# A long convolution and an MLP block on one core: new buffer plan and work order, and the second filter spectrum folded by accumulated matmuls

## The chip, the cores and the metric

The kernel runs on one core of a Trainium2 chip. The metric is device microseconds of one execution. The five engines (TensorE = PE, VectorE = DVE, ScalarE = ACT, GpSimd = POOL, SyncE = SP) each work through a queue of their own in order; SP issues almost all DMAs. A semaphore wait at the head of a queue holds everything behind it.

## What is computed

```
x  = q                                          # 2048 x 512, bf16
kv = (4-tap causal shift of k by shift_k) * v
y  = first 2048 of ifft(fft(kv, 4096) * fft(ssm_k, 4096)) + kv * ssm_D
h  = x + layernorm(x) * y
u  = layernorm(h);  g = gelu(layernorm(u) @ w1)
x1 = u + (g, its four column quarters shifted by -1, +1, -2, +2 rows) @ w2
out = h + x1 + gelu(layernorm(x1) @ w3) @ w4    # w3: 512x1792, w4: 1792x512
```

## The kernel before

**Two halves.** The rows form two halves s = 0, 1 of 1024 rows, each of eight blocks b of 128. The FFT of length 4096 is done as two steps of small matmuls against sine tables. Four signals go forward: the filter's halves F0 and F1, and kv's halves A0 and A1. The first output half needs A0·F0, the second A0·F1 + A1·F0.

**The work calls.** Every call is registered once with a name, its dependencies and a function; a string `ORDER` (lines 31 to 62) lists all calls by number, with the engine letter (P, V = DVE, A = ACT, G = POOL, S = SP) and the PSUM banks. `emit` walks the string, so ORDER alone sets each engine's queue. The names used below:

- convolution, forward: `S1.sig.b.hp` step 1 on PE (line 397, eight 128x32 matmuls of 512 columns, four column groups side by side), `E1` its eviction to SBUF (line 266, 128x1024), `X.sig.g.kl` an SBUF to SBUF transposition by DMA (line 412), `S2.sig.kl` step 2 on PE (line 420), `E2` its eviction. For F1 the eviction is the fold of line 432: it reads the PSUM result and the stored F0 spectrum and writes their difference (real part) or sum (imaginary part), on DVE only.
- kv: `K.g.c` the shift as matmuls with diagonal tables `dg` (line 449), `KV` the product with v (line 457).
- convolution, back: `P.s.kl...` products of spectra on DVE (line 481; 16 for s = 0, 32 for s = 1), `I2.s.kl` inverse step 2 on PE (line 493), `EV` its eviction, `XI.s.kl` DMA (line 503), `I1.s.b` inverse step 1 on PE (line 511).
- gating with q: `Q` statistics (line 516), `Y` normalised q, `H.s.b` the sum h (line 619), `HS` its second moment (line 603 on ACT, 605 on DVE); `uw`, `rr`, `hn` finish the statistics of a pair of blocks, partly on POOL.
- first MLP: `hb` normalised block (line 655 or 653), turned either on PE (`LT`, line 671, then eviction `TE`) or by two DMA writes to DRAM and a transposing DMA back (`LT`, `TE` at lines 664 and 666 on SP); `W.s.p.h` the matmul with w1 (line 700), `U` its gelu, `X2.s.b` the shifted matmul with w2 (line 729), `S` the sum x1 (line 732), `SS` its second moment, `R` the residual (line 736).
- second MLP: `ux`, `r1`, `xn` statistics, `lb` the normalised block, `LX`/`EX` its turn (PE or DMA), `M.s.p.fp` the matmul with w3 (line 781, seven for a pair p of blocks), `G` its gelu, `O.s.b` the matmul with w4 (line 793), `Z` the last sum (line 795), `OUT` the store (line 797).

**Order before.** PE does all of both convolutions up to `I2.1.3`, with `W.0`, `X2.0.0` to `X2.0.5` between, and then `M.0.0.0`, the first matmul of the second MLP; `I1.1` follows behind the seven `M.0.0`.

**Buffers before.** The large buffers are shared in time. z1 (step 1 results) of A0, F1 and A1 all lie in `r_y`, of F0 in `r_x`; z2/spectrum of A1 and `wv[0]` lie in `r_x`, `wv[1]` in `r_y`. Gelu results G rotate over four homes. Turned blocks have two buffers for the first MLP (`hnT`) and two for the second (`lnT`); normalised blocks two `hbt` and two `lbt`. `Z` writes to two output buffers.

Of the kernel before, what the change touches and what calls it, by code (L numbers as in the profile page):

```python
# [9 lines left out]
P = 128  # L10
# [33 lines left out]
391A0 392P71 394A1 395P6 276P 277V0 413G 414G 393A 396A 368A 278V1 262P4567 281V2 415G 401G 253S 402G 403G 280V3 263A 028S 279P 257S 282P 283M 284A
416V0 399P5 400A 384P4 385A 418S 417V1 419S 286V0 268P0123 420S0 264V 269A 397P7 398A 287V1 289V2 270V 404G0 290V3 265P4501 266A 288P23671 291P 406S
423P5 405A1 292V0 424A 293V1 296V2 267A 294P 421P4 295V3 297P 422A 285S 298A 407S 513P5 302V0 301V1 303P01230 304V2 408S0 305V3 306P 299A 509P4 514V
307V0 308V1 411P5 515A 409P7 510V 511A 310V2 311V3 309P 312P 412A 317V0 410A 521P7 313A 300S 314A 517P6 316V1 320V2 319V3 318P01451 522V 321P 322V0
525P3 337S 573G 574G 575G 579A0 576A1 323V1 325V2 577P70 578A 529P2 580P7 315S 326V3 523A 324P 581A 518V 519A 602G 603G 604G 605G0 327P 329A 328A
582P70 588P6 594P5 430V 431V 429V 584P4 426V 585A 330S 583A 425V 592P1 593A 586P0 427V 589A 587A 428V 432V 433V 590P4 591A 526V 530V 434G 527V 606A1
331P76 332P43 333P21 531A 435V 439G0 595A 516V 440V 599P5 436A1 441A 437V 445G0 442G1 630V 438V 446V 451A0 443V 608S 596P0 631G 632G 607S 609S0 600V0  # L50
601S 460G 461G 334P37 444A 447A 473G 452V 448A1 633V0 635S 610P60 614P1 634V1 611A 616P5 620P6 449V 612P4 450V 457G0 453V 454A1 618P2 615A 462G 466A0
613A 617A 458V 622P7 636S 637S1 638P10 644P5 623A 455V 463V1 464P70 465A 621A 459V 619A 524V 640P4 456V 467P3 645A 646P7 474G 475V 477G1 479S 468V
469P6 471P5 497V 520V 498G 624P3 476A0 499V 478S 528V 480S0 472A 470A 500A1 625V0 502S 533P6 534V 485G 501A0 503S 504S1 537P5 538V 648P3 650P6 649A
539A 535V 483P5 484A 486G 487V 642P3 643A 489V0 491S 481P2 647A 488G1 627P5 658G 659G 660G 482A 512V 597V1 532V 662A0 507P7 490S 492S0 641A 661A1 663S
508A 505P4 495P0 493P7 506A 541P4 545P3 626S 546V 639A 494A 496A 553P7 557P2 561P3 651A 549P6 547A 554V 542V 543A 742V 743G 562V 563A 598S 555A 558V
744V 745A1 550V 569P4 565P7 566V 664S 665S0 666P30 667A 674P2 675A 678P6 652P7 655P3 560V 746V0 748S 628V0 672P5 564V 629S 747S 749S1 676P2 570V 571V
750P40 751A 668P1 669A 548V 756P0 551V 757A 686G 687G 688V 677A 690V0 692S 752P4 753A 689V1 552V 673A 670P1 671A 559V 760P2 761A 762P5 691S 714V 715G
716V 754P4 718G0 717V1 693S0 758P2 759A 694P10 696P0 653V0 654S 704P7 719S 568V 679A 705A 680P2 700P7 540V 695A 536V 763A 702P6 698P5 755A 767P4 720S
656V1 567V 657S 699A 701A 770G 771G 697A 706P7 721S1 722P50 772G 773G0 730P3 774G1 731A 556V 776S 724P1 725A 544V 775S 683P0 684V0 777S0 734P3 703A
764P6 707A 778P70 784P1 685S 728P0 785A 735A 765V0 766S 711P6 681V1 782P1 572V 783A 712V0 713S 682S 732P3 733A 726P6 729A 768V0 769S 727A 708P2 709V1  # L60
710S 723A 788P6 789A 739P5 740V0 741S 790P6 786P4 791A 787A 780P5 781A 736P6 737V0 738S 779A 792P7 793V1 794S 795P6 796V0 797S
# [3 lines left out]
class Plan:  # L65
# [4 lines left out]
    def add(self, name, opts, fn, deps=(), take=(), drop=(), size=0, mode=0, port="", mate=None):  # L70
        n = len(self.t)
        t = dict(mate=mate, n=n, name=name, opts=opts, fn=fn, deps=set(), take=list(take), drop=[], size=size, mode=mode, port=port)
        for d in deps:
            t["deps"].add(self.by[d])
        for d, part, *kind in drop:
            m = self.by[d]
            t["deps"].add(m)
            t["drop"].append((m, kind[0] if kind else self.t[m]["take"][0][0], part))
        self.by[name] = n
        self.t.append(t)  # L80
# [20 lines left out]
def body(ctx, tc, fx, kt, q, v, sd, w1, w2, w3, w4, out):  # L101
# [25 lines left out]
    r_dg = raw("r_dg", DC * 4 * P)  # L127
    w4s = raw("w4s", FC * D)[:].rearrange("p (f d) -> p f d", f=FC)
    z_t = ct("z_t", 2, D, dt=F32)
    hnT = ct("hnT", 2, DC, 256)  # L130

    q_sb = r_q[:].rearrange("p (s b d) -> p s b d", s=2, b=NB)
    fxs = view(r_h, 0, G, "p (s b d) -> p s b d", s=2, b=NB)
# [14 lines left out]
    z1 = {"F0": z1v(r_x), "A0": z1v(r_y), "F1": z1v(r_y), "A1": z1v(r_y)}  # L148
    z2 = {"F0": z2v(r_f0), "F1": z2v(r_f1), "A0": z2v(r_a0), "A1": z2v(r_x)}
    sp = {"F0": spv(r_f0), "F1": spv(r_f1), "A0": spv(r_a0), "A1": spv(r_x)}  # L150
    wv = {0: z1v(r_x), 1: z1v(r_y)}
# [3 lines left out]
    h1T = r_h[:].rearrange("p (c b x) -> p c b x", c=DC, b=NB)  # L155
    h_sb = {0: view(r_v, 0, NB * D, "p (b d) -> p b d", b=NB), 1: view(r_a0, 0, NB * D, "p (b d) -> p b d", b=NB)}
    w1s = view(r_v, NB * D, DC * D, "p (k d) -> p k d", k=DC)
    w2s = view(r_v, NB * D + DC * D, DC * D, "p (k d) -> p k d", k=DC)
    w3s = view(r_k, 0, DC * F, "p (k f) -> p k f", k=DC)
    gbq = [[view(r, lo, 2048, "p (f x) -> p f x", f=8) for lo in (0, 2048)] for r in (r_kv, r_x, r_f0, r_f1)]  # L160

    def gb(i, f, n=1):
        u = f // 8
        r, z = ((0, u), (1 + u, 0), (1 + u, 1), (3, u))[i]
        return gbq[r][z][:, f % 8:f % 8 + n, :]
    lbt = view(r_k, DC * F, 2 * D, "p (i d) -> p i d", i=2)
    obt = [r_kv[:, GS:GS + D], ct("ob1", D)[:]]
# [3 lines left out]
    lnT = r_dg[:].rearrange("p (i c x) -> p i c x", i=2, c=DC)  # L171

    ident = ct("ident", P)
    f1 = ct("f1", 8, 2, 2, 2, 4)
    f2 = ct("f2", 4, 32, 4)
    ftab = ct("ftab", 16, 2, 32)
    ttab = ct("ttab", 8, 3, 64)
    hbt = ct("hbt", 2, D)
    junk = ct("junk", D)
    negpi = ct("negpi", 1, dt=F32)  # L180
    mhalf = ct("mhalf", 8, dt=F32)
    dum = ct("dum", 1, dt=F32)
    qst = ct("qst", 16, 6, dt=F32)
    qmv = ct("qmv", 16, 2, dt=F32)
# [96 lines left out]
    for b in range(4):  # L281
        load(("Lf", 0, b), fxs[:, 0, 2 * b:2 * b + 2, :], fx[0, b].rearrange("p (b d) -> p b d", b=2), size=310)
# [398 lines left out]
    def front(s, p):  # L681
# [8 lines left out]
        if dm:  # L690
            turn("hb", "LT", "TE", "hn", lambda k: hbt[:, k, :], lambda k: hnT[:, k], s, p)
# [154 lines left out]
```

## Time and profile before

| what | us |
|---|---|
| median of 3 runs | 222.65 (221.59 to 222.97) |
| span of the profiled execution | 221.2 |
| PE busy | 200.6, 2372 matmuls |
| DVE busy | 145.3, 320 instructions |
| ACT busy | 134.9, 214 instructions |
| POOL busy | 67.3, 187 instructions |
| moved by DMA | 34.47 MB |

The median lies 1.45 us above the profiled span. An instruction's duration in a row is from its start to its end; back to back, instructions of DVE and ACT overlap by some 0.05 to 0.1 us, so a run of n instructions is taken from the start of the first to the start of what follows ("pace" below). Mean duration of one instruction: fold of line 432 on DVE 681 ns (128x512, 16 of them), 128x1024 eviction (line 266) 1.01 to 1.03 us on ACT and 1.21 to 1.23 us on DVE, product (line 481) 694 ns, w3 matmul 273 ns, w4 matmul 379 ns. DMA landings after issue, median: `X` 3.0 to 4.0 us, `XI` 3.5, block write to DRAM 2.0 to 2.1, transposing DMA 3.1, w3 9.2.

### The profile page before, as it was taken

How to read it: one execution, taken by the hardware profiler on the slowest of the kernel's cores; microseconds unless marked ns; L12 is line 12 of the kernel's file. 1: busy time of each engine (PE TensorE's matmuls, PEld its weight loads, DVE VectorE, ACT ScalarE, POOL GpSimd, SP SyncE). 2: the span in 40 equal slices, each digit the busy share in tenths (PEclk: the TensorE clock that was granted, in tenths of full speed). 3: DMA queues.
4: the chain of work that ended last, by engine and by line, in shares of the span. 5: the costliest groups of instructions: out<-in, count | busy, mean ns of one | idle time of the engine just before them, and what ended most of it. 6: DMA issues, size and time to landing. Idle time of an engine off the chain costs nothing.

```text
span 221.2 us, 5913 instructions
## 1 busy us (share of the span) xinstructions
PE 200.6 (91%) x2372; PEld 118.7 (54%) x2372; DVE 145.3 (66%) x320; ACT 134.9 (61%) x214; POOL 67.3 (30%) x187
## 2 busy tenths in 40 slices
PE   6889578996867799999999999999999999999993
PEld 4454234451223255558548958746588666665641
DVE  7898989999499899899899348059765001312121
ACT  4799889988498979687956646655063323123400
POOL 7342000093276680234685345003125000000000
PEclk9999999999695899999999999999999999999998
DMA  6996798869927535973234154341415402111001
GB/s 193 363 394 271 286 291 318 309 244 307 426 115 268 187 83 160 269 303 98 50 74 95 27 113 102 89 104 46 91 32 142 98 2 45 47 50 47 24 24 47
DMA packets 35996, 34.47 MB, mean 156 GB/s; under 512 B 26753, under 2 KB 28802, under 8 KB 35714
## 3 DMA queue, kind: packets, MB, share of 16 engines
q1 hardware_dynamic: 35970, 34.11, 48.6%
q8 instruction: 18, 0.29, 0.6%
q14 instruction: 8, 0.07, 0.1%
HBM read 13.13 MB, written 5.24 MB: 83 GB/s over the span
## 4 chain that ended last, share of the span: by engine, by line
PE 67%; DMA 11%; SPq 6%; ACT 6%; DVE 5%; issue 2%; POOL 0%; DVEq 0%
PE ps L781 22%; PE ps L793 22%; PE ps L729 6%; PE ps L700 5%; PE ps L493 4%; SPq L412 4%; DMA r_h<-in_fx_dram 3%; SPq L275 3%; DMA r_k<-in_kt_dram 3%; DMA r_x<-r_y 3%; PE ps L511 3%; DVE r_f L432 2%; PE ps L397 2%; ACT r_y L266 2%; DMA r_f<-r_y 2%
## 5 line engine op out<-in xcount | busy, mean ns | idle before, releaser
L781 PE MATMUL ps<-r_dg,r_k 128*128 128x256 bf16 x448 | 51.4, 273 | 0.0
L781 PEld LDWEIGHTS <-r_k 128*128 128x128 bf16 x448 | 43.6, 98 | 7.8 <-issue 0.7
L785 ACT ACTIVATE r_f<-ps 128x512 bf16<-128x512 f32 x26 | 14.9, 598 | 27.8 <-PE ps L781 27.8
L793 PE MATMUL ps<-w4s,r_f 128*128 128x512 bf16 x104 | 24.1, 379 | 0.0
L481 DVE TENSOR_TENSOR r_p<-r_a,r_f 128x1024 bf16<-128x1024 bf16 x32 | 20.8, 694 | 1.0 <-PE ps L493 0.9
L266 ACT CAST r_y<-ps 128x1024 bf16<-128x1024 f32 x19 | 18.6, 1022 | 4.6 <-PE ps L397 4.1
L493 PE MATMUL ps<-r_p,ttab 32*32 32x512 bf16 x768 | 15.8, 379 | 1.4 <-ACT r_x L266 0.6
L700 PE MATMUL ps<-hnT,r_v 128*128 128x256 bf16 x128 | 16.5, 281 | 0.5 <-DMA hnT<-dhb 0.5
L795 DVE TENSOR_TENSOR r_kv<-ps,r_v 128x512 bf16<-128x512 f32 x5 | 3.4, 686 | 20.5 <-PE ps L793 20.5
L795 DVE TENSOR_TENSOR r_kv<-ps,r_a 128x512 bf16<-128x512 f32 x6 | 4.2, 692 | 19.3 <-PE ps L793 17.3
L449 PE MATMUL ps<-r_dg,r_k 128*128 128x256 bf16 (+3 forms) x112 | 15.8, 288 | 1.0 <-ACT r_dg L314 0.5
L785 ACT ACTIVATE r_x<-ps 128x512 bf16<-128x512 f32 x16 | 9.2, 599 | 12.2 <-PE ps L781 12.2
L793 PEld LDWEIGHTS <-r_f 128*128 128x128 bf16 x104 | 10.2, 98 | 11.8
L266 ACT CAST r_vs<-ps 128x1024 bf16<-128x1024 f32 (+1 forms) x12 | 14.3, 1228 | 2.4 <-PE ps L493 1.9
L700 PEld LDWEIGHTS <-r_v 128*128 128x128 bf16 x128 | 12.5, 100 | 5.1 <-issue 2.0
L793 PE MATMUL ps<-w4s,r_x 128*128 128x512 bf16 x64 | 15.1, 379 | 0.0
L729 PE MATMUL ps<-r_v,r_h 128*128 128x512 bf16 x64 | 15.0, 380 | 0.0
L449 PEld LDWEIGHTS <-r_k 128*128 128x128 bf16 x112 | 9.5, 98 | 8.9 <-issue 4.6
L266 ACT CAST r_x<-ps 128x1024 bf16<-128x1024 f32 x14 | 13.7, 1017 | 0.7 <-PE ps L397 0.4
L397 PEld LDWEIGHTS <-f 128*32 128x32 bf16 x256 | 6.2, 99 | 12.6 <-issue 7.3
L493 PEld LDWEIGHTS <-ttab 32*32 32x32 bf16 x768 | 8.3, 88 | 8.7 <-issue 6.0
L793 PE MATMUL ps<-w4s,r_kv 128*128 128x512 bf16 x56 | 12.6, 379 | 0.0
(180 smaller groups left out, 343.8 us busy)
## 6 DMA issues: line engine op xcount, KB each, us to landing
r_k<-in_kt_dram SPq DMA_DIRECT2D x8, 259.0 KB, 5.6
r_h<-in_fx_dram SPq DMA_DIRECT2D x8, 256.0 KB, 4.9
r_v<-in_v_dram SPq DMA_DIRECT2D x4, 512.0 KB, 6.2
r_q<-in_q_dram SPq DMA_DIRECT2D x8, 256.0 KB, 6.4
r_f<-r_x SPq DMA_DIRECT2D x8, 256.0 KB, 3.0
r_a<-r_y SPq DMA_DIRECT2D x8, 256.0 KB, 3.5
r_x<-r_vs SPq DMA_DIRECT2D x4, 512.0 KB, 3.5
r_f<-r_y SPq DMA_DIRECT2D x8, 256.0 KB, 4.0
```

Source lines behind the costliest of these rows:

```text
L266: (act.copy if e in "AM" else on[e].tensor_copy)(o, i)
L397: nc.tensor.matmul(ps[32 * j:32 * j + 32, sl[hh], :], lhsT=f1t[:, 4 * t + 2 * hp + hh, :], rhs=src(2 * b + b0), start=True, stop=True)
L412: nc.sync.dma_start(z2[sig][g:P:2, kl, :, :], z1[sig][kl:P:4, 2 * g:2 * g + 2, :, :])
L449: nc.tensor.matmul(o[:, (d + j0) * P:(d + j1 + 1) * P], lhsT=kT[s][c][:, bb, x:x + P], rhs=diag[:, c, j0:j1 + 1, :].rearrange("p j x -> p ...
L481: on[e].tensor_tensor(out=prs[:, sl[0], :, :], in0=sp[a][:, kl, t, :, :], in1=gv, op=MUL)
L493: nc.tensor.matmul(ps[c:c + 32, bk[h], :], lhsT=ttab[32 * h:32 * h + 32, 2 * kl + t, 2 if x else xx, 32 * b0:32 * b0 + 32], rhs=prs[32 * h ...
L700: nc.tensor.matmul(ps[:, sl[0], j * 256:(j + 1) * 256], lhsT=w1s[:, k, m * P:(m + 1) * P], rhs=hnT[:, k_, k, :], start=(k == 0), stop=(k = ...
L729: nc.tensor.matmul(ps[:, sl[0], :], lhsT=h1T[:, m, bb, x:x + P], rhs=w2s[:, m, :], start=(m == 0), stop=(m == DC - 1))
L781: nc.tensor.matmul(ps[:, sl[0], j * 256:(j + 1) * 256], lhsT=w3s[:, k, fc * P:(fc + 1) * P], rhs=lnT[:, k_, k, :], start=(k == 0), stop=(k ...
L785: act.activation(gb(gi, 2 * fp, 2), ps[:, got(("M", s, p, fp))[0], :].rearrange("p (j x) -> p j x", j=2), ACT.Gelu_apprx_tanh)
L793: nc.tensor.matmul(ps[:, sl[0], :], lhsT=gb(gi, fc)[:, 0, (b % 2) * P:(b % 2 + 1) * P], rhs=w4s[:, fc, :], start=(fc == 0), stop=(fc == FC ...
L795: add(("Z", s, b), {V: 0.61}, lambda e, sl, b=b: vec.tensor_tensor(out=obt[sl[0]], in0=ps[:, got(("O", s, b))[0], :], in1=h_sb[s][:, b, :] ...
```

## The change

1. **The fold.** A table `f1g` is built from `f1`: for each pair of cosine and sine columns, (-second, first). Step 1 of F1 takes two sources: the F1 rows with `f1`, and in the same PSUM accumulation the F0 rows with `f1g`. The F1 spectrum then comes out of step 2 already folded; the 16 folds on DVE are gone, and its eviction is an ordinary `E2` copy. F1's step 1 has 16 matmuls a call instead of 8: 64 more.
2. **Buffers.** `r_x`, `r_y` become `r_a1`, `r_z`; `wv[0]`, `wv[1]` and A1's z1 lie in `r_z`, A1's z2 in `r_a1`. F0's source rows have a buffer of their own (later w1 and w2), F1's lie in the second half of q's, so the loads of q's second half wait for F1's step 1. h lies in v's buffer for both halves, `Z` writes in place. Gelu homes go from four to eight places behind six locks; the homes of the first and third pair lie in v's second half, so `I1.1.0` waits for the `O` of these two pairs. The turned blocks share three buffers `xT`, the normalised ones four, across both MLPs.
3. **The h1T buffer** is split into halves, with `ed0` and `ed1` copying the two edge columns that the other half needs, and `edge0`, `edge1` the zero columns.
4. **The turn** of the pairs (0,2) and (0,3) of the first MLP goes from DMA to PE: 16 more transposing matmuls, four `TE` copies; four writes and two transposing DMAs fewer.
5. **ORDER** is new as a whole (804 calls against 798). PE's queue reaches `M.0.0.0` before `S2.F1.3`, `I2.1.2` and `I2.1.3`, which now stand between the matmuls of the second MLP; `I1.1` stands between the `M.0.2`. Of the eight `E2.F1`, six halves of a spectrum go to ACT, two to DVE. The pairs of the second MLP go in the order (0,1), (0,2), (0,0), (0,3) for the choice of homes only.

The core of the diff (without ORDER and renamed buffers):

```diff
-    z1 = {"F0": z1v(r_x), "A0": z1v(r_y), "F1": z1v(r_y), "A1": z1v(r_y)}
-    z2 = {"F0": z2v(r_f0), "F1": z2v(r_f1), "A0": z2v(r_a0), "A1": z2v(r_x)}
-    wv = {0: z1v(r_x), 1: z1v(r_y)}
+    z1 = {"F0": z1v(r_f1), "A0": z1v(r_a1), "F1": z1v(r_a1), "A1": z1v(r_z)}
+    z2 = {"F0": z2v(r_f0), "F1": z2v(r_f1), "A0": z2v(r_a0), "A1": z2v(r_a1)}
+    wv = {0: z1v(r_z), 1: z1v(r_z)}
...
+    def f1turn(e, sl):
+        x, y = (z[:].rearrange("p a i c j k -> p (a i) c (j k)") for z in (f1, f1g))
+        if e == V:
+            vec.tensor_scalar(out=y[:, :, 0, :], in0=x[:, :, 1, :], scalar1=-1.0, scalar2=None, op0=MUL)
...
+        on[e].tensor_copy(y[:, :, 1, :], x[:, :, 0, :])
...
-    def step1(b, hp, src):
+    def step1(b, hp, *srcs):
         def f(e, sl):
             for hh in range(2):
-                for t in range(2):
-                    for b0 in range(2):
-                        j = 2 * t + b0
-                        nc.tensor.matmul(ps[32 * j:32 * j + 32, sl[hh], :], lhsT=f1t[:, 4 * t + 2 * hp + hh, :], rhs=src(2 * b + b0), start=True, stop=True)
+                for i, (src, tab) in enumerate(srcs):
+                    for t in range(2):
+                        for b0 in range(2):
+                            j = 2 * t + b0
+                            nc.tensor.matmul(ps[32 * j:32 * j + 32, sl[hh], :], lhsT=tab[:, 4 * t + 2 * hp + hh, :], rhs=src(2 * b + b0),
+                                             start=(i == 0), stop=(i == len(srcs) - 1))
...
-                if sig == "F1":
-                    def fold(e, sl, n=n, kl=kl, t=t):
-                        for r, op in ((0, SUB), (1, ADD)):
-                            vec.tensor_tensor(out=sp[sig][:, kl, t, r, :], in0=ps[:, got(n)[2 * t + r], :], in1=sp["F0"][:, kl, t, 1 - r, :], op=op)
...
-    BYDMA = {("hb", 0, 2), ("hb", 0, 3), ("hb", 1, 1), ("hb", 1, 2), ("hb", 1, 3), ("lb", 0, 1), ("lb", 0, 2), ("lb", 0, 3),
+    BYDMA = {("hb", 1, 1), ("hb", 1, 2), ("hb", 1, 3), ("lb", 0, 1), ("lb", 0, 2), ("lb", 0, 3),
```

PE's queue around the first matmul of the second MLP, in call names (from the two ORDER strings):

```
before: ... X2.0.4 LX.0.0 X2.0.5 LX.0.1 I2.1.3.2 I2.1.3.3 M.0.0.0 M.0.0.3 ... M.0.0.4 I1.1.0 I1.1.1 I1.1.2 O.0.1 O.0.0 I1.1.3 M.0.1.0
after:  ... X2.0.5 LX.0.0 S2.A1.3 LX.0.1 X2.0.2 M.0.0.0 S2.F1.3 M.0.0.3 ... M.0.0.4 I2.1.2.0 I2.1.2.1 O.0.0 I2.1.2.2 I2.1.2.3 O.0.1 I2.1.3.0 M.0.1.0
        I2.1.3.1 ... M.0.1.6 I2.1.3.2 I2.1.3.3 O.0.3 O.0.2 M.0.2.0 I1.1.0 M.0.2.6 I1.1.1 M.0.2.1 I1.1.2 ... LT.1.0 M.0.2.5 LT.1.1 I1.1.3 W.1.0.1
```

## Prediction

> **What bounds it now.** First the shares by engine and the slices in time, then the chain, then the stretches.
>
> ```profile
> PE 200.6 (91%) x2372; PEld 118.7 (54%) x2372; DVE 145.3 (66%) x320; ACT 134.9 (61%) x214; POOL 67.3 (30%) x187
> ...
> PE   6889578996867799999999999999999999999993
> ...
> DVE  7898989999499899899899348059765001312121
> ACT  4799889988498979687956646655063323123400
> ...
> PEclk9999999999695899999999999999999999999998
> ```
>
> PE has holes in the first 14 slices (77 us) and none later; DVE and ACT are as full there as PE. The shares over the span hide that.
>
> ```profile
> 56.19 1.89 PE ps L511 x8
> ...
> 100.18 6.22 PE ps L781 x56
> 106.40 2.70 PE ps L511 x24
> ...
> 208.42 9.08 PE ps L793 x42
> 217.50 0.02 issue
> 217.52 0.69 DVE r_kv L795
> ```
>
> In the chain, PE runs without a wait from M.0.0.0 (100.18) to its last matmul (217.52): 117.3 us. So the end is the start of M.0.0.0, plus the PE work behind it, plus a tail of 221.2 − 217.5 = 3.7.
>
> ```profile
> 0.00:20.00 20.00, 16.55 (x176) 9.45 (x180) 16.51 (x52) 15.65 (x25) 9.62 (x58) 1.00 0.83 296
> 20.00:40.00 20.00, 15.38 (x300) 6.59 (x292) 18.38 (x23) 17.44 (x19) 0.22 (x1) 1.00 0.86 304
> 40.00:60.00 20.00, 16.73 (x336) 7.32 (x330) 17.53 (x30) 15.23 (x16) 8.25 (x18) 0.91 0.87 323
> 60.00:80.00 20.00, 15.07 (x272) 7.03 (x268) 17.84 (x40) 18.01 (x33) 13.92 (x35) 0.83 0.53 185
> 80.00:100.00 20.00, 19.37 (x491) 10.65 (x488) 18.68 (x34) 16.41 (x27) 5.89 (x14) 1.00 0.69 215
> ```
>
> (Stretch, PE, weight load, DVE, ACT, POOL busy, clock, DMA.) PE idles 3.45 + 4.62 + 3.27 + 4.93 + 0.63 = 16.9 us before 100. To this come slow-clock pieces of the chain: at 56.19 eight matmuls of line 511 take 1.89, later 0.97 (+0.9); 58 us: 16 of line 397 take 1.74 instead of 1.05 (+0.7); 69.8: line 700 1.86 instead of 1.05 (+0.8); two S2 1.06 instead of 0.63 (+0.9). In all 3.3. Lost: 20.2; pure PE work before M.0.0.0: 100.2 − 20.2 = 80.0. From 20 to 100 DVE is busy 72.4 of 80 us (0.905), ACT 67.1 (0.84): these two decide when M.0.0.0 can start.
>
> **The change, PE.** Added: 64 matmuls of S1.F1. Eight of line 397 take 0.50 to 0.55 us in the chain (16 in 1.00, 8 in 0.55), so 8 x 0.52 = +4.2. No row accumulates two passes in line 397's four column groups. At least 0, if they all fill holes (they take PE time, so no gain); 64 x 379 ns = 24.3, if none ran beside another. I take 4.2: I2 (line 493) accumulates in groups of 32 columns and 32 of its matmuls take 0.55. Four more LT at 0.22: +0.9. Moved behind M.0.0.0: I2.1.2 and I2.1.3 (four times 64 matmuls at 1.09 = 4.4) and S2.F1.3 (0.6): −5.0. So before M.0.0.0 there are 80.1 us, as before; behind it 117.3 + 5.0 = 122.3. The break-even is M.0.0.0 at 217.5 − 122.3 = 95.2.
>
> **The fold.** A fold of 1024 columns is two of the 681 ns rows, pace 1.24; the copy that takes its place has pace 1.14 on DVE (three of line 266 from 19.65 to 23.05), 0.92 on ACT. So DVE loses 8 x 1.24 and gets 2 x 1.14 back, −7.6; ACT gets 6 x 0.92 = +5.5. The rule against the change is in the Trainium skill, TensorEngine Tiling (Array Packing), section PSUM Bottleneck: tiling speeds TensorE up but not the emptying of PSUM. The rows agree that this work stays; what is gained is that ACT may do it. By the rule alone, PE's 4.2 would be pure loss: +4.2.
>
> **When M.0.0.0 can start.** It needs EX.0.0 (ACT) and EX.0.1 (DVE). Up to 22.9, where ACT starts on E2.F0 (the first cast to r_f), the loads and KV set the pace; one q load now stands before the last k load, another before the second v load, and the k rows land up to 2 us later (9.9 to 12, at 0.85 us per 256 KB), but the last A0 steps come out at 22 to 23 again, since fewer E1.F0 are left then. I count from 22.9 in both. The `f1g` table is two small DVE instructions (line 316's pace 0.16 to 0.19 for 128x128), 0.35, while DVE waits for k: 0, or 0.35 without that cover.
>
> ACT's queue from there to EX.0.0: 47 evictions x 0.92 = 43.2; 8 U x 0.49 = 3.9; 7 squares x 0.74 = 5.2; 3 scalings x 0.72 = 2.2; 2 copies x 0.49 = 1.0; gelu table 1.4. Sum 56.9: without a gap it ends at 79.8, with the busy share of before (0.84) at 90.7.
>
> DVE's queue to EX.0.1: 33 products x 0.60 = 19.8; 9 evictions x 1.14 = 10.3; 8 KV x 0.615 = 4.9; 7 Q x 0.61 = 4.3; 8 H and 4 S x 0.75 = 9.0; 3 moments x 0.83 = 2.5; 8 turned copies x 0.38 = 3.0; R, three hb, Y 2.3; the small statistics 4.6. Sum 60.7: gapless 83.6, at share 0.905 90.0.
>
> So M.0.0.0 starts between 84 and 91, given 0.5 for PE to get there. PE alone allows 80.1 + 3.4 (the first idle stretch) = 83.5. I take 88.5, above the middle, as neither queue was ever gapless. Before, DVE had all 32 P.1 and eight folds in front; now 15 P.1 stand behind, with I2.1.2 and I2.1.3 under M.0.0 and M.0.1. P.0 shows the gain first: DVE gets to P.0.3 with two KV and one EV between instead of seven KV, two E1 and four Q, so I1.0.0 should start near 48 to 50 instead of 56.19.
>
> **Clock.** After idles of 1.71 and 2.21 us the granted clock of 5 us stretches fell to 0.66 and 0.63. The Trainium skill, TensorE: Matmul & The Clock Gate, Part 1, asks for an idle window of about 3.4 us; here shorter holes in a row sufficed. By the rule none of the 3.3 us would come back; I keep it inside the shares above.
>
> **Behind M.0.0.0.** Counting PE work against the chains:
> - P.1.2 and P.1.3: I2.1.3.2 is reached 22 us after M.0.0.0, DVE has its products at 19. Hidden; each us of DVE beyond 3 is on the path.
> - `ed1` on POOL waits for all P.1 and the U.0.3; behind it r1.0.2, xn.0.2 and lb.0.5 wait, for EX.0.4 and M.0.2.0. It holds them to 19; EX.0.4 lands at 27, PE comes at 29.
> - `ed0` waits for U.1.0, with rr.1.3, hn.1.3 and TE.1.6 behind it. A DMA turn takes 5.7 us from the first write's issue to landing (107.75, transposition issued 110.37, +3.1). TE.1.6 lands near 53.5, PE wants W.1.3 at 52.5: 1 us.
> - I1.1.0 waits for four O that PE did just before: 0. XI.1.3, behind EX.0.4 on SP, lands at 28, PE comes at 30.
> - Three instead of four turned buffers: EX.1.2 must land between X2.1.2 and M.1.1.0, with 11.6 us of PE work between. The chain S, SS, ux, r1, xn, lb (0.75 + 0.74 + 0.65 + 1.0 + 0.6 + 0.8, two S in front) and 5.7 make some 12; before, from X2.1.0's end (144.5) to EX.1.0's landing (155.94 + 3.1) it was 14.6. So 0.5 to 3 us.
> - X.F0.1.2 stands on SP behind the last E1.F0 (ACT, after three sine tables), with Lv.1.1 and the other X.F0 behind it; S2.F0 comes 6 us later: 0. If that cover is gone, 1 to 2 us, inside the shares.
> - Z in place, zero columns, two DMA turns fewer: not on the chain, 0; SP has 2 x 1.2 + 4 x 0.4 us less to issue.
>
> Sum of waits: 0 to 5, I take 1.5. Span 88.5 + 122.3 + 1.5 + 3.7 = 216.0, and 1.45 for the median's distance: 217.5, 2.3% less.
>
> **Rivals.**
> - No difference: M.0.0.0 comes at 90, but the DMA turns in front of W.1.2, W.1.3, M.1.1 and M.1.2 are each late as before's 14.6 us suggest, together 5 us. 90 + 122.3 + 5 + 3.7 + 1.45 = 222.4. For it: the five slacks are under 1 us. Against: no turn held PE for more than 0.5 us before.
> - Slower: ACT becomes the bound. It takes the new copies, and E1.A1 now waits for I1.0, which shares r_z. At the busy share of ACT's worst stretch (15.23 of 20, 0.76), EX.0.0 comes at 22.9 + 56.9/0.76 = 97.8, and 98.3 + 122.3 + 1.5 + 3.7 + 1.45 = 227.3. It makes the kernel over 1% slower once M.0.0.0 is later than 95.2 − 1.5 + 2.2 = 95.9. Against: the wait of 3.09 us at 59 in that stretch was for I1, which now comes earlier.
> - The added pass does not run beside itself: up to +20 us, near 237. Against: I2's row.
>
> **Chances.** Forecast (M.0.0.0 at 84 to 91, waits to 3) 0.64; no difference 0.17; slower by ACT 0.15, by serial matmuls 0.04. Low end 84 + 122.3 + 3.7 + 1.45 = 211.5; high end M.0.0.0 at 93 and 4.5 of waits, 225. One per cent is about what a measurement tells from none; faster 0.64, within 0.17, slower 0.19.
>
> **What would show it.** S1.F1 calls at 1.0 to 1.1 us; I1.0.0 near 49 (later than 54: the P.0 step is wrong); ACT's idle from 23 to M.0.0.0 below 11 us; M.0.0.0 at 84 to 91; then no wait on PE over 3 us. Wrong if M.0.0.0 comes after 95, or PE waits over 5 us behind it.

## The result and the profile after

| what | before | after |
|---|---|---|
| median of 4 runs each, us | 222.47 (221.59 to 222.97) | 228.51 (227.41 to 231.02) |
| ratio, 95% interval | | 1.0276 (1.0221 to 1.0332) |
| span of the profiled execution, us | 221.2 | 226.6 |
| start of `M.0.0.0`, us | 100.18 | 96.12 |
| from there to the end of the last matmul, us | 117.3 | 126.8 |

The kernel became 2.8% slower. `M.0.0.0` starts 4 us earlier, where 11.7 had been forecast, and the stretch behind it is 9.5 us longer, where 6.5 had been forecast with its waits. Runs over 1.5% above the fastest of their kernel are left out of the ratios here and of the medians in the table below, and the profiled executions of e2_sd_early_act, e5_v_early and e6_grouped are such runs, so that only what does not depend on that is read from them.

The page of the changed kernel, its shares by engine and its slices of 5.7 us:

```profile
PE 203.1 (90%) x2452; PEld 118.9 (52%) x2452; DVE 146.1 (64%) x350; ACT 131.5 (58%) x204; POOL 62.5 (28%) x160
...
PE   7099976799869989999999999989998999999993
...
DVE  7377997789699998998966288726897000005321
ACT  3666998979799976985543389134753375500000
...
PEclk9979999999999999999999999999999999999999
```

The second slice of PE is a 0, where before had an 8: for 5 us PE does nothing at all, at the very start. DVE has a hole there too (3, before 8). The clock is full in all slices but the third, so the slow-clock pieces round 75 us are gone, and the time is lost all the same.

The chain of waits shows what stood at the start (start, duration, what):

```profile
1.64 4.07 DMA r_fx<-in_fx_dram
5.73 5.01 DMA r_vs<-in_sd_dram
10.76 0.42 DVE r_fx L299
11.22 2.75 PE ps L403 x13
...
195.73 27.21 PE ps L791 x126
222.96 0.69 DVE r_v L793
```

`r_vs<-in_sd_dram` is `Lsd`, the load of `ssm_D`: 1 KB. It is issued when a 256 KB load of filter rows has landed (1.64 + 4.07 = 5.71), and takes 5.01 us itself. Line 299 is `dr`, which adds `ssm_D` to the first filter row, and `S1.F0.0.0` on PE waits for it. The instructions of this place, with the idle time before them and what ended it in brackets:

```profile
5.73 0.50 ACTq L276 DMA_DIRECT2D r_vs<-in_sd_dram  x1
10.76 0.41 DVE L299 TENSOR_TENSOR r_fx<-r_fx,r_vs 1x512 bf16<-1x512 bf16 x1 [3.12 <-DMA r_vs<-in_sd_dram]
11.22 2.75 PE L403 MATMUL ps<-r_fx,f 128*32 128x512 bf16 x24 [5.36 <-DVE r_fx L299]
```

The load stands on ACT's queue. Before, SP issued it at 3.06 us as the sixth of its loads, and DVE came to `dr` at 9.91 without waiting. In ORDER this is one letter of one word, `000S` to `000A`. The prediction does not mention it.

The stretches of 20 us up to `M.0.0.0` (PE, weight load, DVE, ACT, POOL busy; clock, DMA share, GB/s):

```profile
0.00:20.00 20.00, 13.37 (x125) 7.27 (x126) 12.39 (x44) 12.08 (x18) 11.74 (x63) 0.91 0.76 248
20.00:40.00 20.00, 16.16 (x293) 7.65 (x295) 17.39 (x23) 16.18 (x17) 2.36 (x5) 1.00 0.84 286
40.00:60.00 20.00, 16.54 (x381) 8.00 (x369) 15.96 (x33) 16.74 (x17) 3.17 (x3) 1.00 0.65 209
60.00:80.00 20.00, 17.75 (x309) 8.57 (x307) 19.09 (x57) 19.60 (x31) 15.64 (x28) 1.00 0.69 232
80.00:100.00 20.00, 18.81 (x317) 11.43 (x315) 19.26 (x38) 15.65 (x25) 2.13 (x9) 1.00 0.65 270
```

In the first stretch PE does 3.2 us less than before (16.55), DVE 4.1 less, ACT 3.6 less. From 60 to 80 ACT is busy 19.60 of 20 us and DVE 19.09: that work is dense now, but it came late. The prediction counted from ACT's first cast to `r_f`, and took it at 22.9 as before. Here it is at 27.77; the second row is `EX.0.0` on ACT, for which `M.0.0.0` waits, as for `EX.0.1` on DVE, which ends at 95.97:

```profile
27.77 3.86 ACT L262 CAST r_f<-ps 128x1024 bf16<-128x1024 f32 x4
...
94.31 0.59 ACT L262 COPY r_dg<-ps 128x512 bf16<-128x512 bf16 x1
```

Behind `M.0.0.0`, PE's timeline:

```profile
126.02 1.04 PE L778 MATMUL ps<-xtx,r_k 128*128 128x256 bf16 x8
127.00 1.04 PE L512 MATMUL ps<-r_z,f 64*128 64x512 bf16 x8
127.97 1.05 PE L778 MATMUL ps<-xtx,r_k 128*128 128x256 bf16 x8
128.95 1.04 PE L512 MATMUL ps<-r_z,f 64*128 64x512 bf16 x8
129.92 1.05 PE L778 MATMUL ps<-xtx,r_k 128*128 128x256 bf16 x8
...
151.32 1.92 PE L703 MATMUL ps<-r_dg,r_fx 128*128 128x256 bf16 x16 [0.81 <-DMA r_dg<-dhb]
...
172.71 3.67 PE L778 MATMUL ps<-r_dg,r_k 128*128 128x256 bf16 x32 [0.88 <-DMA r_dg<-dlb]
...
176.82 1.05 PE L778 MATMUL ps<-xtx,r_k 128*128 128x256 bf16 x8 [0.44 <-DMA xtx<-dlb]
```

Two things are new. Eight `M` (line 778, whole array) and eight `I1` (line 512, tiles of 64 rows) that take turns start 0.97 to 0.98 us apart; among themselves eight `M` take 0.87, and eight `I1` 0.90 in before's 24 in 2.70. And three DMA turns come late: from the start of the row before by its pace, PE stands 0.97, 1.04 and 0.62 us there.

### The profile page after: what moved, and what is told of

The parts are those of the page before. It is cut to its first block, busy times and chain, and to the rows that moved or that the text cites. A ratio compares the mean times of both kernels' runs of the same rounds, so it can differ in the third digit from the quotient of the medians.

```text
span 226.6 us, 6041 instructions
## 1 busy us (share of the span) xinstructions
PE 203.1 (90%) x2452; PEld 118.9 (52%) x2452; DVE 146.1 (64%) x350; ACT 131.5 (58%) x204; POOL 62.5 (28%) x160
## 4 chain that ended last, share of the span: by engine, by line
PE 55%; DMA 15%; DVE 12%; issue 6%; ACT 5%; SPq 3%; POOL 2%; DVEq 0%; ACTq 0%; POOLq 0%
PE ps L791 20%; PE ps L778 14%; PE ps L726 5%; PE ps L494 4%; PE ps L403 3%; PE ps L703 3%; DMA r_a<-r_a 3%; DVE r_v L622 2%; DMA r_vs<-in_sd_dram 2%; DMA r_v<-in_v_dram 2%; ACT r_a L262 2%; SPq L419 2%; PE ps L450 2%; DMA r_dg<-dlb 2%; DMA r_fx<-in_fx_dram 2%
## 5 line engine op out<-in xcount | busy, mean ns | idle before, releaser
L793 DVE TENSOR_TENSOR r_v<-ps,r_v 128x512 bf16<-128x512 f32 x16 | 10.8, 685 | 42.4 <-issue 30.3
L778 PE MATMUL ps<-r_dg,r_k 128*128 128x256 bf16 x280 | 32.8, 273 | 1.0 <-DMA r_dg<-dlb 0.9
L262 ACT CAST r_a<-ps 128x1024 bf16<-128x1024 f32 (+1 forms) x23 | 25.1, 1130 | 4.8 <-PE ps L403 3.2
L262 ACT CAST r_f<-ps 128x1024 bf16<-128x1024 f32 (+1 forms) x19 | 19.4, 1063 | 7.5 <-PE ps L403 7.0
L778 PE MATMUL ps<-xtx,r_k 128*128 128x256 bf16 x168 | 20.7, 273 | 0.4 <-DMA xtx<-dlb 0.4
L622 DVE SCALAR_TENSOR_TENSOR r_v<-ps,qsd,z_t 128x512 bf16<-128x512 f32 x16 | 11.4, 747 | 6.4 <-PE ps L512 6.1
L729 DVE SCALAR_TENSOR_TENSOR r_q<-r_v,hrr,ps 128x512 bf16<-128x512 bf16 x16 | 11.6, 742 | 5.3 <-PE ps L726 5.1
L703 PEld LDWEIGHTS <-r_fx 128*128 128x128 bf16 x128 | 12.0, 98 | 4.3 <-issue 1.3
L619 POOL TENSOR_SCALAR z_t<-r_q,qrs,qnm 128x512 f32<-128x512 bf16 x13 | 10.3, 796 | 12.2 <-DVE r_v L622 11.0
L791 PE MATMUL ps<-w4s,r_a 128*128 128x512 bf16 x56 | 12.7, 379 | 0.0
```

Source lines behind the costliest of these rows:

```text
L262: (act.copy if e in "AM" else on[e].tensor_copy)(o, i)
L622: vec.scalar_tensor_tensor(out=h_sb[s][:, b, :], in0=ps[:, got(("I1", s, b // 2))[b % 2], :], scalar=qsd[:, i:i + 1], in1=z_t[:, got(("Y", ...
L703: nc.tensor.matmul(ps[:, sl[0], j * 256:(j + 1) * 256], lhsT=w1s[:, k, m * P:(m + 1) * P], rhs=xt[:, k, :], start=(k == 0), stop=(k == DC ...
L729: vec.scalar_tensor_tensor(out=q_sb[:, s, b, :], in0=h_sb[s][:, b, :], scalar=hrr[:, 4 * s + b // 2, 0, b % 2:b % 2 + 1], in1=ps[:, got((" ...
L778: nc.tensor.matmul(ps[:, sl[0], j * 256:(j + 1) * 256], lhsT=w3s[:, k, fc * P:(fc + 1) * P], rhs=xt[:, k, :], start=(k == 0), stop=(k == D ...
L791: nc.tensor.matmul(ps[:, sl[0], :], lhsT=gb[:, fc, (b % 2) * P:(b % 2 + 1) * P], rhs=w4s[:, fc, :], start=(fc == 0), stop=(fc == FC - 1))
```

## The experiments

In all kernels below, both controls among them, the transposing DMAs are plain DMAs of the same 256 KB in pieces of 256 bytes, so that the blocks which go by that way stay unturned.

```diff
-        nc.sync.dma_start_transpose(
-            xT[sl[0]].rearrange("p c x -> p (c x)"), d[:].rearrange("c p x -> (c p) x")),
+        nc.sync.dma_start(
+            xT[sl[0]].rearrange("p c (h x) -> p (c h) x", h=2), d[:].rearrange("c (h p) x -> p (c h) x", h=2)),
```

| kernel | median (runs), us | ratio to before, 95% | profiled, us | `M.0.0.0` | to last matmul |
|---|---|---|---|---|---|
| c_before | 220.10 (7) | 0.9951 (0.9903 to 0.9999) | 220.10 | 97.21 | 117.4 |
| c_after | 227.63 (2) | 1.0284 (1.0182 to 1.0387) | 226.87 | 95.31 | 125.7 |
| e1_sd_sp | 224.25 (4) | 1.0118 (1.0028 to 1.0207) | 223.77 | 91.69 | 126.4 |
| e4_no_fold_mm | 232.14 (4) | 1.0500 (1.0441 to 1.0558) | 232.17 | 97.74 | 128.1 |
| e2_sd_early_act | 224.31 (7) | 1.0219 (1.0115 to 1.0323) | 227.70 | 104.78 | 117.4 |
| e3_mm_fold_alone | 229.15 (4) | 1.0301 (1.0240 to 1.0362) | 229.44 | 106.35 | 117.6 |
| e5_v_early | 222.45 (9) | 1.0072 (1.0016 to 1.0128) | 225.14 | 93.76 | 125.7 |
| e6_grouped | 224.94 (6) | 1.0136 (1.0086 to 1.0186) | 227.91 | 94.07 | 128.2 |
| e7_sd_act_first | 224.35 (4) | 1.0158 (1.0093 to 1.0224) | 224.34 | 93.27 | 125.4 |
| f1_fill_i1 | 223.04 (10) | 1.0125 (1.0088 to 1.0161) | 222.80 | 91.06 | 126.1 |
| f2_fill_late | 222.78 (11) | 1.0084 (1.0053 to 1.0114) | 222.49 | 91.12 | 125.7 |
| f3_table_later | 221.06 (12) | 1.0021 (0.9986 to 1.0057) | 220.91 | 90.79 | 124.5 |

Each ratio is to runs of the kernel before that were made beside it, so the difference of two kernels by their ratios is not quite that of their medians (up to 1.8 us apart below).

**The controls.**

> Control: the kernel before with its 12 transposing DMAs replaced by plain DMAs of the same 256 KB between the same places (256-byte pieces; the two-block turns are left out, so those blocks enter the matmuls unturned). PE never waited long for a turn here: 222 to 223 us, as before.

> Control: the changed kernel with its 10 transposing DMAs replaced by plain DMAs of the same size (the turns of these blocks are left out). All theories: the start up to M.0.0.0 at 96 is untouched; a plain DMA lands about 1 us earlier, so the waits of 0.8, 0.9 and 0.4 us at the turns shrink: 226.5 to 228.5 us, still 1.5 to 2.5% above the kernel before.

The difference is still there with plain DMAs: 7.5 us between the medians, where the two kernels with the transposing ones differ by 5.7. c_before came 2 us under what was expected of it, c_after as expected, but its median rests on two runs. So the experiments can be made on these two, and a difference to c_after is good to about 1 us.

**The load of ssm_D back on SP.** One letter of ORDER:

```diff
-000A
+000S
```

> As c_after (turns left out), with one word of ORDER altered: the 1 KB load of ssm_D (Lsd) is issued by SP, second in its queue, instead of by ACT. Theory A (the late ssm_D row, landed at 10.7 us, holds DVE and then PE for 5 us and moves everything behind it): the first step 1 of block 0 starts near 7 instead of 11.2 us, M.0.0.0 comes 4 to 5 us earlier (91 to 92), and the kernel is 4 to 5 us faster than c_after. Rival B (the 64 added matmuls are the loss): the start is earlier but PE is full later on, 0 to 1 us faster than c_after. Rival C (the new order is held by v's loads, which SP issues late, and by DMA turns): 1 to 2 us faster than c_after.

224.25, that is 3.4 us below c_after (3.1 by the profiled executions, 3.7 by the ratios): more than rivals B and C give, less than theory A's 4 to 5. The timeline of e1_sd_sp at the start, with idle time and its end in brackets:

```profile
1.17 0.32 SPq L276 DMA_DIRECT2D r_vs<-in_sd_dram  x1
...
7.53 0.41 DVE L299 TENSOR_TENSOR r_fx<-r_fx,r_vs 1x512 bf16<-1x512 bf16 x1
...
7.99 1.48 PE L403 MATMUL ps<-r_fx,f 128*32 128x512 bf16 x24 [1.60 <-DVE r_fx L299]
```

SP issues the load at 1.17, `dr` runs at 7.53 without a wait for it, and PE starts on `S1.F0.0.0` 3.2 us earlier than in the changed kernel. `M.0.0.0` comes 3.6 us earlier than in c_after, at 91.69, just outside the forecast's 84 to 91. This one word holds a little under half of the 7.5 us; some 4 us against c_before remain. By the profiles they arise behind `M.0.0.0`: it comes 5.5 us earlier than in c_before, and from there to the last matmul it takes 9.0 us more, of which 4.8 are the calls that were moved there.

**The same load on ACT in the old order.** The opposite edit in c_before:

```diff
-000S
+000A
```

> c_before with one word of ORDER changed: the 1 KB load of ssm_D (Lsd) is issued by ACT instead of SP, at the same place in the order. At that place its completion counter has no earlier user, so that ACT issues it right after its sines, at about 2.7 us (c_before: SP at 3.05, and dr, which needs it, at 9.81 without waiting for it). Theory A1 (in the changed kernel the load was late because it had to wait for the counter of a slower load, issue 5.73, and then stood behind the loads that were issued before it): issued at about 2.7 it lands before 9.8, dr stays at 9.8, the time is that of c_before, 220.8, within 1 us. Theory A2 (a small load that ACT issues lands late as such, 5 us or more behind the loads of SP, wherever it stands): it lands at 8 to 10.5, dr at up to 10.5, the time 220.8 to 221.8.

224.31, 4.2 us above c_before (5.9 by the ratios). Neither theory's issue time came: in e2's timeline ACT comes to the load only behind four evictions,

```profile
4.67 3.76 ACT L268 CAST r_x<-ps 128x1024 bf16<-128x1024 f32 x4
...
9.72 0.50 ACTq L282 DMA_DIRECT2D r_vs<-in_sd_dram  x1
...
13.74 0.41 DVE L305 TENSOR_TENSOR r_h<-r_h,r_vs 1x512 bf16<-1x512 bf16 x1 [3.98 <-DMA r_vs<-in_sd_dram]
14.21 1.04 PE L399 MATMUL ps<-r_h,f 128*32 128x512 bf16 x8 [2.26 <-DVE r_h L305]
```

It stands from 8.43 to 9.72 at the issue itself, and the 1 KB lands 4.0 us after it. The program's list of instructions has, for this issue as for that of the changed kernel, a wait on the completion counter of an earlier load: the loads of all queues use eight counters in turn, and here the issue waits for counter 7. In the changed kernel it is counter 2, that of SP's third load, the 256 KB of filter rows in the chain above. So the place in the queue, the counter and the landing add up, and the load costs 3.4 us in the new order and 4 to 6 in the old one.

**The load first on ACT.** This tells the queue from the counter and the backlog:

```diff
+    act.dma_start(drow[0:1, :], sd)
     vec.memset(wup, 0.0)
...
-    add("Lsd", {SP: 0.42, A: 0.5}, lambda e, s: (nc.sync if e == SP else nc.scalar).dma_start(drow[0:1, :], sd), size=16)
+    add("Lsd", {SP: 0.42, A: 0.5}, lambda e, s: None, size=16)
```

> c_after with the 1 KB load of ssm_D still issued by ACT, but as the first instruction of its queue, ahead of the load of ACT's table; there its completion counter has no earlier user and no other load is under way (c_after: the load waits for the counter of a 256 KB load, is issued at 5.73 and lands behind the loads issued before it). Theory A1 (wait for the counter and the backlog make it late, not the queue): issued at about 0.8, dr at 7.5 and the first matmuls of S1.F0.0 at 8.0 as in e1_sd_sp; time that of e1_sd_sp, 223.5 to 225. Theory A2 (a small load that ACT issues lands late wherever it stands): landing after 9, time 226 to 229.4.

224.35, as e1_sd_sp. In its timeline the load is issued at 0.71 and `dr` no longer waits:

```profile
0.71 0.51 ACTq L210 DMA_DIRECT2D r_vs<-in_sd_dram  x1
...
7.84 0.41 DVE L300 TENSOR_TENSOR r_fx<-r_fx,r_vs 1x512 bf16<-1x512 bf16 x1
```

Theory A1 holds: ACT's queue as such is not slow. What counts is that the load is issued before the others and waits for none of them. How the counter's wait and the landing behind the other loads share the cost was not separated.

**The fold undone.** e1_sd_sp with the eight folds on DVE again and one source in F1's step 1:

```diff
-    forward1("F1", [(fb, f1t), (f0, f1gt)],
+    forward1("F1", [(fb, f1t)],
...
+                if sig == "F1":
+                    def fold(e, sl, n=n, kl=kl, t=t):
+                        for r, op in ((0, SUB), (1, ADD)):
+                            vec.tensor_tensor(out=sp[sig][:, kl, t, r, :], in0=ps[:, got(n)[2 * t + r], :], in1=sp["F0"][:, kl, t, 1 - r, :], op=op)
```

> As e1_sd_sp, with the fold undone: step 1 of F1 takes F1's rows alone, and all eight folds run on DVE, at the places of ORDER where the evictions stood. Theory A: within 2 us of e1_sd_sp, slower rather than faster, since DVE gets 7.6 us more before M.0.0.0 and PE 4.2 less. Rival B: 3 to 4 us faster than e1_sd_sp.

232.14, 7.9 us above e1_sd_sp. In this order the fold by matmuls is a gain, and a larger one than either theory gave. The stretch from 60 to 80 us, with the columns of the table above, of e1_sd_sp and then of e4:

```profile
60.00:80.00 20.00, 17.57 (x332) 9.48 (x328) 19.48 (x51) 18.77 (x25) 12.37 (x24) 1.00 0.67 239
...
60.00:80.00 20.00, 13.91 (x202) 6.86 (x202) 17.96 (x48) 11.07 (x17) 9.60 (x21) 0.83 0.57 194
```

and a row of its PE timeline in that stretch, with the idle time ahead of it:

```profile
66.84 1.21 PE L403 MATMUL ps<-r_kv,f 128*32 128x512 bf16 x8 [2.20 <-DVE r_f L439]
```

ACT works 11.07 us where e1_sd_sp has 18.77: the work for ACT is not there in time, because PE waits for DVE (line 439 is the fold), and PE's clock is 0.83 there, 1.00 in e1_sd_sp. The eight folds stand on DVE in an order that was made without them, so the 7.9 us are not the price of the folds in the best order for them.

**The fold alone, in the old order.** c_before with the same pass and table, the folds gone, four evictions `E2.F1` on ACT and four on DVE:

```diff
-    forward1("F1", fb,
+    forward1("F1", [(fb, f1t), (f0, f1gt)],
...
-    add("f1", {V: 0.01}, lambda e, sl: None)
+    add("f1", {V: 0.36}, lambda e, sl: f1fn[0](V, sl))
```

> c_before with change 2 alone: the second filter spectrum's fold by step-1 matmuls with the turned table (built by DVE at the place of f1), the eight folds of DVE gone and the eight evictions E2.F1 in their place, four on ACT and four on DVE; order, memory plan and queues stay. Theory A (the fold by matmuls is no cause of the loss, and e4_no_fold_mm, 7.9 us slower than e1_sd_sp, holds in the old order too, though that order was made with DVE's folds in it and the evictions stay at their places): 217 to 221, against c_before's 220.8; S1.F1 8 x 0.5 us longer on PE, DVE's wait for folds gone, M.0.0.0 no later than in c_before (97.2). Rival B (the 64 more matmuls stand on the path): +3 to +4.2, 224 to 225, M.0.0.0 at 100 to 101.

229.15, 9.0 us above c_before (7.8 by the ratios): theory A falls, and rival B's 4.2 is too small. The issues of the four `XI.0` on SP's timeline, first in c_before:

```profile
34.83 0.58 SPq L505 DMA_DIRECT2D r_x<-r_vs  x1
42.10 0.56 SPq L505 DMA_DIRECT2D r_x<-r_vs  x1
46.54 0.56 SPq L505 DMA_DIRECT2D r_x<-r_vs  x1
49.05 0.56 SPq L505 DMA_DIRECT2D r_x<-r_vs  x1
```

and the same in e3:

```profile
37.76 0.58 SPq L512 DMA_DIRECT2D r_x<-r_vs  x1
46.98 0.56 SPq L512 DMA_DIRECT2D r_x<-r_vs  x1
51.60 0.56 SPq L512 DMA_DIRECT2D r_x<-r_vs  x1
54.41 0.56 SPq L512 DMA_DIRECT2D r_x<-r_vs  x1
```

They fall behind by 2.9, 4.9, 5.1 and 5.4 us. In the old order six of the eight `S1.F1` calls stand on PE between the first `I2.0` and the second, and now take 5.4 us there instead of 3.5. `I1.0.0` then waits for evictions of ACT, which has four more of them, and comes 7.3 us later (61.08 for 53.75), `M.0.0.0` 9.1. Not all of it is shown to be the fold's. The first of these issues is 2.9 us late, and so is the first `I2.0` on PE (34.57 for 31.43), before a single matmul of `S1.F1` has run. In e3's timeline of PE stands ahead of them

```profile
26.95 1.40 PE L435 MATMUL ps<-r_a,ftab 64*32 64x512 bf16 x32 [1.79 <-DMA r_a<-r_y]
...
29.95 1.89 PE L458 MATMUL ps<-r_dg,r_k 128*128 128x512 bf16 x7
```

a wait for the landing of `X.A0`, 0.38 and 0.64 us in c_before, and then seven matmuls that take 1.89 us where c_before has 1.04: the granted clock is 0.50 from 28 to 34 us, 1.00 in c_before. The profile of the kernel before has nearly the same wait without this fold (1.72 us, at 27.95), with the clock at 1.00 behind it. So of the 9 us some 3 may have nothing to do with the fold, and it costs 6 to 9 in the old order; how they divide between PE and ACT was not separated. Fold and order belong together all the same: the fold alone costs these 6 to 9 us, the order without the fold, with the new buffers, 12.0 (e4 against c_before), all together 4.2 (e1 against c_before).

**The loads of v and k earlier.** e1_sd_sp with four loads ahead of the turning transfers on SP, in call names:

```diff
-X.F0.0.0 X.F0.0.2 Lk.1.1 Lk.1.0 X.F0.0.1 X.F0.1.2 X.F0.1.1 X.F0.1.0 Lv.1.1 ... X.A0.1.2 Lv.1.0
+Lv.1.1 Lv.1.0 Lk.1.1 Lk.1.0 X.F0.0.0 X.F0.0.2 X.F0.0.1 X.F0.1.2 X.F0.1.1 X.F0.1.0 ... X.A0.1.2
```

> e1_sd_sp with four words moved forward on SP: the second halves' loads Lv.1.1, Lv.1.0, Lk.1.1, Lk.1.0 are issued before X.F0.0.0 instead of behind it, so that they start while SP has nothing to do (in e1_sd_sp SP stood from 7.1 to 10.97 at X.F0.0.0 and issued Lv.1.1 at 18.05, Lv.1.0 at 27.11; PE waited 1.44 us for KV.3.0's v and 0.63 for KV.2.0's). Theory A (the turning transfers at the head of SP's queue hold up the loads, and that is a part of what is left of the loss): both waits go, step 2 of A0 starts up to 1.5 us earlier, I1.0.0 at 52 to 53 (53.87), the time 1 to 2.5 us below e1_sd_sp, 222 to 223.2. Rival B (1.5 MB more in the same 20 us only makes the turning transfers land later): S2.F0 and S2.A0 start 1 to 2 us later, and the time is that of e1_sd_sp (224.25) or up to 1.5 us above. Rival C (other waits take over): early waits gone, I1.0.0 unchanged within 0.5, same time.

222.45, in theory A's range, 1.8 us below e1_sd_sp by the medians, 1.0 by the ratios; the intervals overlap, so the size is not settled. The waits for v's second half are gone; DVE has one of 1.24 us for v's first half instead, at 16.36.

**Tiled matmuls in fewer stretches.** e1_sd_sp with three calls moved:

```diff
-I2.1.2.0 I2.1.2.1 O.0.0 I2.1.2.2 I2.1.2.3
+I2.1.2.0 I2.1.2.1 I2.1.2.2 I2.1.2.3 O.0.0
...
-I2.1.3.0 M.0.1.0 I2.1.3.1
+I2.1.3.0 I2.1.3.1 M.0.1.0
...
-I1.1.0 M.0.2.6 I1.1.1
+I1.1.0 I1.1.1 M.0.2.6
```

> e1_sd_sp with three words moved: O.0.0 behind I2.1.2.3, I2.1.3.1 next to I2.1.3.0, I1.1.1 next to I1.1.0, so that behind M.0.0.0 the matmuls in tiles (S2, I2, I1) stand in seven stretches instead of ten. Theory A (each change between whole matmuls and matmuls in tiles costs PE about 0.1 us: eight M take 0.96 to 0.98 beside a tiled stretch and 0.87 among themselves): from M.0.0.0 to the last matmul 0.6 us less than in e1_sd_sp (126.4 with its waits), 224.25 goes to 223.6. Rival B (the longer starts are a pipeline effect that is made good later): the same 126.4 and the same time. Rival C (the order moved earlier finds its inputs not ready): a wait in front of I2.1.3.1 or I1.1.1 of 0.3 us or more.

224.94, 0.7 us above e1_sd_sp with intervals that overlap: no gain in the time. In the profile theory A and rival C are both there. The same six groups of `M` and `I1` that took 5.84 us in e1_sd_sp (121.60 to 127.44) take 5.62 here (125.47 to 131.09), two of `I1` and two of `M` now one behind the other,

```profile
126.44 1.90 PE L512 MATMUL ps<-r_z,f 64*128 64x512 bf16 x16
128.27 1.92 PE L778 MATMUL ps<-xtx,r_k 128*128 128x256 bf16 x16
```

and those round `I2.1.3.0` and `I2.1.3.1` 7.32 instead of 7.51: 0.2 us for each of these two stretches saved. But two of the calls of `I2.1.2`, moved forward, now wait for their products, in e6's timeline of PE,

```profile
103.12 1.01 PE L494 MATMUL ps<-r_p,ttab 32*32 32x512 bf16 x40 [1.03 <-DVE r_p L482]
104.32 0.62 PE L494 MATMUL ps<-r_p,ttab 32*32 32x512 bf16 x24 [0.19 <-DVE r_p L482]
```

which, with DMA turns that came some 0.5 us later, is more than was saved: from `M.0.0.0` to the last matmul it is 128.2 us, 126.4 in e1_sd_sp.

**Work into the remaining waits.** Three kernels, each on top of the one before. f1_fill_i1 is e5_v_early with two calls moved:

```diff
-I1.0.0 S1.A1.0.0 I1.0.1 S1.A1.0.1
+S1.A1.0.0 S1.A1.0.1 I1.0.0 I1.0.1
```

> e5_v_early with the first two calls S1.A1.0.0 and S1.A1.0.1 put in front of I1.0.0 on PE, which in e5_v_early stood idle for 2.02 us in front of I1.0.0, waiting for the landing of XI.0.3; their evictions stay behind I1.0.0, whose input they overwrite. Theory A (PE's order counts here): the 1.1 us of the two calls lie in the wait, I1.0.1 follows I1.0.0 1.1 us earlier, M.0.0.0 0.5 to 1.1 us earlier, 221.4 to 222. Rival B (from 60 to 92 us DVE and ACT, 19 of 20 us busy, set the pace): the calls lie in the wait, M.0.0.0 stays within 0.3 us and so does the time, 222.2 to 222.8.

223.04, no gain: rival B, though 0.2 us above its range. From 60 to 80 us DVE is busy 19.45 and ACT 18.27 of 20 us; ahead of such a stretch, filling a hole of PE brought nothing. (`M.0.0.0` of e5's profiled execution, 93.76, is no measure here.)

f2_fill_late, in the same manner; `I2.1.3.1` and `I1.1.1` are also put beside their neighbours as in e6_grouped, and the four calls named last in its text moved to fit:

```diff
-M.1.1.1 M.1.2.0 M.1.1.2 M.1.2.3 ... M.1.2.5 O.0.6 M.1.0.3
+M.1.1.1 M.1.1.2 O.0.6 M.1.2.0 M.1.2.3 ... M.1.2.5 M.1.0.3
...
-W.1.3.1 W.1.3.0 X2.1.3 X2.1.2
+X2.1.2 W.1.3.1 W.1.3.0 X2.1.3
```

> f1_fill_i1 with the waits behind M.0.0.0 filled: O.0.6 (13 matmuls, 3.0 us, so far at the end) and M.1.1.2 in front of M.1.2.0, which waited 0.5 to 1.5 us for the landing of EX.1.4; X2.1.2 in front of W.1.3.1, which waited 0.4 to 0.9 us; I2.1.3.1 next to I2.1.3.0 and I1.1.1 next to I1.1.0 (two tiled stretches fewer, 0.2 us each by e6_grouped); R.0.6, Z.0.6, Z.0.4 and OUT.0.6 moved to fit. Theory A (these waits are gone without new ones): 1.3 to 2.5 us less than f1_fill_i1, from M.0.0.0 to the last matmul 123.5 to 124.3 where e1_sd_sp had 126.3; 219.5 to 221. Rival B (what comes next in the same queue is late instead): 0 to 0.8 less.

222.78, rival B again. `O.0.6` took a wait of 1.23 us away, but `X2.1.2`, in f2's timeline of PE, waited itself:

```profile
146.88 0.82 PE L726 MATMUL ps<-r_fx,r_f 128*128 128x512 bf16 x3 [1.24 <-ACT r_f L707]
```

f3_table_later puts `X2.1.2` back and moves ACT's table load:

```diff
-glu ... S1.F1.0.0 S1.F1.1.1 E1.F1.1.1 S1.F1.0.1 E1.F1.0.1
+... S1.F1.0.0 S1.F1.1.1 E1.F1.1.1 S1.F1.0.1 E1.F1.0.1 glu
```

> f2_fill_late with two things changed. X2.1.2 stays at its old place behind W.1.3.0: in f2_fill_late it waited 1.24 us itself, for U.1.1 on ACT, in place of the 0.4 us it was to fill. And ACT loads its table (word glu, 1.28 us and a first 0.2 us call) behind the last evictions of E1.F1 instead of ahead of two of them, into the 1.25 us in which ACT waits for I1.0.0; S1.A1.0.1 waited 1.34 to 1.45 us for the slots of those two evictions. Theory A (both waits go): S1.A1.0.1 follows S1.A1.0.0 at once, I1.0.0 starts when XI.0.3 lands, at about 52.2 instead of 53.2 to 53.3; from M.0.0.0 to the last matmul 124.4 instead of 125.6; time 1.2 to 2.2 us less than f2_fill_late, 220.6 to 221.6, level with c_before's 220.8 in spite of the 4.9 us of tiled matmuls that stand behind M.0.0.0 here. Rival B (DVE and ACT set the pace from 60 to 92 us): the early part gains nothing at M.0.0.0, the late part 1.2: 221.5 to 221.8.

221.06, ratio 1.0021 (0.9986 to 1.0057): level with before, 1.0 us above c_before's median. The late part came as said (124.45 us from `M.0.0.0` to the last matmul, 124.4 forecast). `I1.0.0` came at 52.29 instead of 53.28, but `M.0.0.0` only 0.33 us earlier (90.79). No version here beats both kernels.

## Why the prediction was wrong

The forecast was 217.5 us, at most 225; it came to 228.51. Its steps:

- **"The last A0 steps come out at 22 to 23 again" failed.** They came at 27, and the cast from which both queues were counted at 27.77 instead of 22.9: 4.9 of the 10.6 us by which the profiled span, 226.6, missed the sum of 216.0. The step priced the new order of the q, k and v loads, and left out the one load that had changed its queue. `dr` and `S1.F0.0.0` wait for those 1 KB, and everything on PE stands behind. With the load back on SP the cast comes at 23.96 and the kernel is 3.4 us faster; e2 shows the same cause with the sign turned, and e7 that it is the load's place behind the others, not the queue.
- **"X.F0.1.2 stands on SP ... 0" was too small.** The price of a lost cover, 1 to 2 us, was in the text, and the cover was gone: `Lv.1.1` and `Lv.1.0` came behind the turning transfers, and `KV` waited: 0.42 us for v's second half in the changed kernel, 1.44 in e1_sd_sp. e5_v_early has 1.0 to 1.8 us for it, with the doubt named above.
- **`I1.0.0` at 48 to 50 failed**: 57.61, and 52.29 in the best of the kernels here. The step counted what DVE has in front of `P.0.3`. What held was the sequence landing of `X.A0`, `S2`, `P`, `I2`, `XI`, with 4 us of a transfer in it. The text had named 54 as the sign that this step is wrong.
- **`M.0.0.0` at 84 to 91** failed too: 96.12, beyond the break-even of 95.2 that the text gave. The sums of the two queues were right: from 27.77 to 95.50 ACT is busy 58.3 us and DVE 60.3, for 56.9 and 60.7. But 88.5 asked both to run denser than before (0.87 and 0.93), and they did not: 56.9 of the 67.1 us to the end of `EX.0.0`, 0.85, and 60.7 of the 68.2 to the end of `EX.0.1`, 0.89. That is the other 2.7 of the 7.6 us by which `M.0.0.0` was late. With the load in place it comes at 91.69 in e1_sd_sp and 90.79 in f3, at the late end of the range.
- **The stretch behind it, 122.3 and 1.5 of waits, was mis-sized** by the last 3.0 of the 10.6. Measured 126.8 = 117.4 + 4.8 of moved work + 3.0 of waits + 1.6. The moved work was right (four `I2` at 1.07 and `S2.F1.3` at 0.55). The waits were twice the 1.5 taken, within the 0 to 5 given. The last 1.6 us, what is left of the measured time, were in no term: the moved calls stand in ten stretches between whole-array matmuls where before had two, and eight stretches more at 0.2 us each come to as much. The rule that speaks of it is in the Trainium skill, TensorEngine Tiling (Array Packing), section Key Properties: a change of the tiling mode drains TensorE. The prediction cited another section of that page as the rule against the change. The rows above agree with this one, at 0.2 us a stretch.
- **The fold's price on PE was right**: a call with 16 matmuls takes 0.86 to 1.05 us (1.0 to 1.1 forecast), four side by side in 0.215, so the rival of serial matmuls falls. The gain of moving it off DVE was right in sign in the new order (7.9 us in e4_no_fold_mm, more than the sum of instruction times); in the old order it is a loss.
- **The rival "slower" came to the right place by another way.** It had `M.0.0.0` past 95.9 through ACT as the bound. ACT was busy 19.6 of 20 us from 60 to 80, but it had been idle before that, for want of work: in the first 20 us it did 12.08 where before had 15.65.
- **"No difference" by late DMA turns** had 5 us for them; they took some 2.6 of the 3.0.

## What to carry to other kernels

When a whole order is replaced, list every call whose queue letter changed, however small, and ask of each what it now stands behind and who waits for it; a 1 KB load that no sum would notice cost 3.4 us here. An order and a kernel's balance of work are made for each other: the fold by matmuls gained 7.9 us in one order and cost 6 to 9 in the other, so a part of such a change tested alone says little about the whole. When short tiled calls are strewn among whole-array matmuls to fill PE, count the changes of mode too, and check that PE is what sets the pace where a hole is filled.

## What the runs showed of the hardware

- A small load can take as long as a large one: 1 KB landed 5.01 us after its issue in the changed kernel and 4.0 us in e2_sd_early_act, behind 256 KB loads that had been issued before it.
- In this program a load's issue can wait for another engine's load, since both use the same one of eight completion counters: ACT stood from 2.64 to 5.73 us until SP's third load had landed, at 5.71.
- A change between whole-array and tiled matmuls and back costs about 0.2 us: eight `M` in 0.97 to 0.98 instead of 0.87, eight `I1` in 0.97 instead of 0.90, and 0.22 and 0.19 us won back for each of two stretches joined in e6_grouped.
- PE's granted clock can fall behind short holes, and need not: in e3_mm_fold_alone it was 0.50 from 28 to 34 us, behind a wait of 1.79 us, and in the profile of the kernel before it stayed at 1.00 behind one of 1.72 us at 28. No rule for it follows from these runs, and it was not tested by itself.
